# Full-width PE shapes, other FFN step budgets and a rotated PSUM set for the last FFN pair, in a fused attention and SwiGLU kernel

## The chip, the cores and the metric

One Trainium2 chip; the program runs on one of its cores. A time is device microseconds of one launch, the median of several executions. The engines are named as the profile names them: PE (TensorE's matmuls; PEld is its weight loads), ACT (ScalarE), DVE (VectorE), POOL (GpSimd, which here also issues the loads of q, k and v) and SP (which issues the loads of the weights and the stores of the result).

## The reference, cut to what matters

Causal attention with a decay from a running sum, on 8 batches with 8 heads of 576 rows and 64 columns, and then a normalised SwiGLU feed-forward layer (FFN) on the 4608 rows of 512 columns that the heads give together.

```python
scores = (1 / np.sqrt(64)) * q @ k.transpose(0, 1, 3, 2)
cum = np.cumsum(np.maximum(s, 0.0), axis=-1)
scores = np.where(causal, -1e9, scores + np.minimum(-(cum[..., :, None] - cum[..., None, :]), 0.0))
x = (softmax(scores) @ v).transpose(0, 2, 1, 3).reshape(4608, 512)
xn = x / np.sqrt(np.mean(x * x, axis=-1, keepdims=True) + 1e-06) * rms_g
g, val = xn @ w_gate, xn @ w_val            # 512 x 1536 each
out = (g / (1 + np.exp(-g)) * val) @ w_out  # 1536 x 512
```

## The kernel before, in words

The 64 heads n (8 of each batch) are written in a loop (lines 298 to 316). A row of 576 is cut in five chunks, four of 128 and one of 64 (`CS`, line 19). For each head:

- `emit_load` (157): POOL issues three loads (q, k, v) into one of three fixed staging tiles, two heads ahead. A load reads 640 rows, so it takes 64 rows of the next head too (not so for the last head).
- `emit_te` (178), one head ahead: ten transposes on PE (185, 187) put q and k into PSUM with 65 rows; the row more carries the running sum. DVE copies qt (190), ACT copies kt (191), 576 columns each.
- `emit_spv` (194): for each chunk jb of keys, the scores (209; their columns are the queries from 128·jb on: 512 and 64, 448, 320, 192, 64), exp on ACT into `pt` (211), and a select on POOL that zeroes the upper triangle of the diagonal block (214). Scores have two PSUM buffers ("s"). Then for each of five chunks i of queries the value matmuls (222), 15 in all, with `pt` as the loaded operand and v as the 65 moving columns; the last column gives the denominators. DVE inverts these (228) and scales into the x tile of the batch (229). For the last chunk jb = 4 only 64 rows are used, and for i = 4 only 64 columns are loaded.

After the eighth head of a batch, `emit_batch_tail` (233) normalises its five x tiles on DVE, with a logarithm and an exp on ACT. After every second batch a generator `ffn_pair_steps` (248) is queued, which writes the FFN of two batches (T = 1152 rows) in 55 steps: 10 transposes of x (257, 260); 36 gate steps, which for each of 12 blocks fb of 128 hidden columns take the rows in groups of 512, 512 and 128 (four matmuls for the gate into pg, 267; tanh on ACT, 270; four for the value into pvl, 273; on DVE uscr = (tanh + 1)·pg, 276, and h = uscr·pvl, 279); and 9 output blocks of 12 matmuls into py (286), a copy on ACT (289) and a store (290). pg, pvl and py share two PSUM buffers ("f"). The loop writes four steps after each head while a generator is queued; what is left is written after the last head.

What is written is not the order on the chip: a planner in the framework orders each engine's instructions when the kernel is compiled, by its own costs and by what is ready, and it takes what is written earlier first. Each engine then runs its instructions in that fixed order, and waits by semaphores. Buffers of a pool tile are handed on when all who use them are done.

## Time and profile before

| | before |
|---|---|
| median of 4 runs | 622.77 us (622.17 to 622.98) |
| profiled execution, and its span | 622.17 us; 620.4 us |
| PE busy, share of the span | 520.1 us, 84% |
| DVE | 350.9 us, 57% |
| ACT | 325.4 us, 52% |
| POOL | 257.6 us, 42% |
| chain that ended last | PE 47%, issue 15%, POOL 13%, ACT 11%, DVE 9% |
| granted TensorE clock, mean | 0.952 of 2.4 GHz |

The span counts from the first instruction to the last; the profiled execution took 1.8 us more than it. Busy time of PE is modelled at its end (matmuls overlap), so single matmuls look longer (379 ns on average for an output matmul) than the distance between two of them. The chain of waits goes back from the last instruction, at each step to what released it; "issue" is time in which an engine waited for nothing that the profile shows. No engine's share tells what bounds the kernel, since the stages differ: heads alone, gate steps beside heads, output blocks, and a last FFN pair alone.

### The profile page before, as it was taken

How to read it: one execution, taken by the hardware profiler on the slowest of the kernel's cores; microseconds unless marked ns; L12 is line 12 of the kernel's file. 1: busy time of each engine (PE TensorE's matmuls, PEld its weight loads, DVE VectorE, ACT ScalarE, POOL GpSimd, SP SyncE). 2: the span in 40 equal slices, each digit the busy share in tenths (PEclk: the TensorE clock that was granted, in tenths of full speed). 3: DMA queues.
4: the chain of work that ended last, by engine and by line, in shares of the span. 5: the costliest groups of instructions: out<-in, count | busy, mean ns of one | idle time of the engine just before them, and what ended most of it. 6: DMA issues, size and time to landing. Idle time of an engine off the chain costs nothing.

```text
span 620.4 us, 10789 instructions
## 1 busy us (share of the span) xinstructions
PE 520.1 (84%) x3733; PEld 290.8 (47%) x3733; DVE 350.9 (57%) x1261; ACT 325.4 (52%) x671; POOL 257.6 (42%) x523
## 2 busy tenths in 40 slices
PE   0078878979999999799989998799989995777797
PEld 0045555545555545455545545455545452333343
DVE  5345565667787703767877407667877126555510
ACT  2475676656676624656676426467766342222221
POOL 4167768665565503475565306465563010000000
PEclk9999999989998998789989997699989996999999
DMA  9997759556555535285556425465552220000012
GB/s 244 295 173 50 49 36 61 33 38 40 38 36 36 39 90 90 17 54 33 39 33 40 60 102 50 27 44 34 38 36 14 71 86 0 2 0 2 0 57 97
DMA packets 134534, 35.42 MB, mean 57 GB/s; under 512 B 127248, under 2 KB 127248, under 8 KB 134480
## 3 DMA queue, kind: packets, MB, share of 16 engines
q0 software_dynamic: 125808, 15.72, 40.3%
q1 hardware_dynamic: 8672, 19.03, 8.7%
q8 instruction: 29, 0.48, 0.3%
q14 instruction: 25, 0.20, 0.1%
HBM read 40.99 MB, written 9.44 MB: 81 GB/s over the span
## 4 chain that ended last, share of the span: by engine, by line
PE 47%; issue 15%; POOL 13%; ACT 11%; DVE 9%; DMA 4%; POOLq 0%; SPq 0%; DVEq 0%; ACTq 0%
PE pg L267 14%; PE pvl L273 8%; PE py L286 8%; PE ps L209 6%; PE pv L222 5%; POOL stk L176 4%; DVE uscr L276 4%; ACT tscr L270 4%; POOL pt L214 4%; ACT pt L211 3%; POOL stq L176 3%; DMA wgs<-in_moe_w_gate_dram 3%; POOL stv L176 2%; PE pq L185 2%; PE pk L187 2%
## 5 line engine op out<-in xcount | busy, mean ns | idle before, releaser
L211 ACT ACTIVATE pt<-ps,cum_T 128x512 bf16<-128x512 f32 (+5 forms) x384 | 170.9, 479 | 92.2 <-PE ps L209 86.1
L267 PE MATMUL pg<-xT,wg_sb 128*128 128x512 bf16 (+1 forms) x576 | 126.6, 339 | 12.8 <-DVE uscr L276 12.0
L214 POOL TENSOR_SCALAR_AFFINE_SELECT pt<-pt 128x128 bf16<-128x128 bf16 (+1 forms) x320 | 91.0, 304 | 93.8 <-ACT pt L211 90.9
L273 PE MATMUL pvl<-xT,wv_sb 128*128 128x512 bf16 (+1 forms) x576 | 120.6, 332 | 5.1 <-DVE h L279 4.9
L209 PE MATMUL ps<-qt,kt 65*128 65x512 bf16 (+5 forms) x384 | 107.4, 323 | 17.7 <-ACT pt L211 16.0
L276 DVE SCALAR_TENSOR_TENSOR uscr<-tscr,pg 128x512 bf16<-128x512 bf16 x144 | 79.5, 552 | 71.5 <-ACT tscr L270 70.4
L228 DVE RECIPROCAL invden<-pv 128x1 f32<-128x1 f32 (+1 forms) x320 | 47.8, 161 | 124.6 <-PE pv L222 116.7
L270 ACT ACTIVATE tscr<-pg 128x512 bf16<-128x512 f32 x144 | 70.4, 489 | 89.6 <-PE pg L267 81.2
L222 PE MATMUL pv<-stv,pt 128*128 128x65 bf16 (+2 forms) x960 | 100.4, 215 | 18.7 <-POOL pt L214 12.7
L222 PEld LDWEIGHTS <-pt 128*128 128x128 bf16 (+2 forms) x960 | 67.8, 112 | 80.5 <-POOL pt L214 26.3
L286 PE MATMUL py<-wo_sb,h 128*128 128x512 bf16 x432 | 93.9, 379 | 0.0
L176 POOL DMA_DIRECT2D stq<-in_q_dram x63 | 54.6, 867 | 88.2 <-DVE stq L167 75.7
L229 DVE TENSOR_SCALAR x<-pv,invden 128x64 bf16<-128x64 f32 (+1 forms) x320 | 82.1, 275 | 1.8
L279 DVE TENSOR_TENSOR h<-uscr,pvl 128x512 bf16<-128x512 bf16 x144 | 78.5, 545 | 6.3 <-PE pvl L273 3.7
L273 PEld LDWEIGHTS <-wv_sb 128*128 128x128 bf16 x576 | 52.1, 100 | 58.1 <-issue 15.0
L267 PEld LDWEIGHTS <-wg_sb 128*128 128x128 bf16 x576 | 50.8, 100 | 56.5 <-issue 28.8
L176 POOL DMA_DIRECT2D stv<-in_v_dram x63 | 54.7, 867 | 42.3 <-PE ps L209 23.5
L176 POOL DMA_DIRECT2D stk<-in_k_dram x63 | 54.8, 869 | 26.5 <-PE pk L187 14.2
L286 PEld LDWEIGHTS <-h 128*128 128x128 bf16 x432 | 42.2, 98 | 50.1
L289 ACT ACTIVATE ysb<-py 128x512 f32<-128x512 f32 x36 | 21.5, 597 | 72.6 <-PE py L286 72.6
L185 PE MATMUL pq<-ident_bf,stq 128*65 128x128 bf16 x320 | 40.3, 251 | 12.4 <-DMA stq<-in_q_dram 10.5
L191 ACT ACTIVATE kt<-pk 65x576 bf16<-65x576 bf16 x64 | 40.9, 639 | 15.6 <-PE pk L187 12.1
(51 smaller groups left out, 333.8 us busy)
## 6 DMA issues: line engine op xcount, KB each, us to landing
out_dram<-ysb SPq DMA_DIRECT2D x36, 256.0 KB, 2.0
stk<-in_k_dram POOLq DMA_DIRECT2D x63, 80.0 KB, 2.9
stv<-in_v_dram POOLq DMA_DIRECT2D x63, 80.0 KB, 2.9
stq<-in_q_dram POOLq DMA_DIRECT2D x63, 80.0 KB, 2.9
wgs<-in_moe_w_gate_dram SPq DMA_DIRECT2D x4, 768.0 KB, 5.4
wvs<-in_moe_w_val_dram SPq DMA_DIRECT2D x4, 768.0 KB, 6.5
wos<-in_moe_w_out_dram SPq DMA_DIRECT2D x12, 256.0 KB, 6.4
cumB<-in_s_dram SPq DMA_DIRECT2D x1, 144.0 KB, 7.9
```

Source lines behind the costliest of these rows:

```text
L176: nc.gpsimd.dma_start(out=st[:, :, 0:D], in_=_head_src_ap(src, n, True))
L209: nc.tensor.matmul(ps[0:cs, 0 : a1 - a0], lhsT=kt[:, i0 : i0 + cs], rhs=qt[:, a0:a1], start=True, stop=True)
L211: nc.scalar.activation(out=pt[0:cs, OFF[jb] + a0 - i0 : OFF[jb] + a1 - i0], in_=ps[0:cs, 0 : a1 - a0], func=AF.Exp, bias=cum_T[0:cs, jb, n ...
L214: nc.gpsimd.affine_select(out=pt[0:cs, OFF[jb] : OFF[jb] + cs], in_=pt[0:cs, OFF[jb] : OFF[jb] + cs], pattern=[[1, cs]], compare_op=ALU.is ...
L222: nc.tensor.matmul(pv[0:ti, :], lhsT=pt[0 : CS[jb], OFF[jb] + 128 * (i - jb) : OFF[jb] + 128 * (i - jb) + ti], rhs=stv[0 : CS[jb], jb, :], ...
L229: nc.vector.tensor_scalar(out=x_tiles[b][i][0:ti, h * D : (h + 1) * D], in0=pv[0:ti, 0:D], scalar1=invden[0:ti, :], scalar2=None, op0=ALU. ...
L267: nc.tensor.matmul(pg[:, 0:gw], lhsT=wg_sb[:, cc, fb * 128 : (fb + 1) * 128], rhs=xT[:, cc, g0:g1], start=(cc == 0), stop=(cc == N_CC - 1))
L270: nc.scalar.activation(out=tscr[:, 0:gw], in_=pg[:, 0:gw], func=AF.Tanh, scale=0.5)
L273: nc.tensor.matmul(pvl[:, 0:gw], lhsT=wv_sb[:, cc, fb * 128 : (fb + 1) * 128], rhs=xT[:, cc, g0:g1], start=(cc == 0), stop=(cc == N_CC - 1))
L276: nc.vector.scalar_tensor_tensor(out=uscr[:, 0:gw], in0=tscr[:, 0:gw], scalar=1.0, in1=pg[:, 0:gw], op0=ALU.add, op1=ALU.mult)
L279: nc.vector.tensor_tensor(out=h_tiles[fb][:, g0:g1], in0=uscr[:, 0:gw], in1=pvl[:, 0:gw], op=ALU.mult)
L286: nc.tensor.matmul(py, lhsT=h_tiles[fc][:, t0 : t0 + 128], rhs=wo_sb[:, fc, :], start=(fc == 0), stop=(fc == N_FC - 1))
```

## The change

Four things are changed. First, PE's shapes: `pt` becomes two fixed tiles with 64 zeroed columns at the end, kt gets all 640 columns, the scores, exp and the value matmuls of the last chunk use 128 rows and columns, with the select still zeroing the rows that don't belong, and x is transposed in full 128 x 128 blocks (its last 64 rows are set to zero once for each batch). Second, in `ffn_steps` the narrow group of 128 rows keeps pg and pvl in one PSUM buffer, and its tanh comes after both. Third, with `deep`, which holds for the last pair alone, pg, pvl and py take their buffers in turn from "f", "s" and "pv". Fourth, the steps are written in two places, two units ahead of `emit_spv` and two after the head (two more if a second generator is queued, and two more from head 48 on); an output block counts as two units. Lines that stay are left out:

```diff
--- before.py
+++ after.py
@@ -148,6 +148,10 @@
                 for i in range(NCH)] for b in range(B)]
...
     h_tiles = [hpool.tile([128, SP], BF16, name=f"h_{fc}", tag=f"h_{fc}") for fc in range(N_FC)]
+
+    pt_slots = [const.tile([128, PT_W + 64], BF16, name=f"pt{s}") for s in range(2)]
+    for s in range(2):
+        nc.vector.memset(pt_slots[s][:, PT_W : PT_W + 64], 0.0)
...
     teed = {}
@@ -186,18 +190,18 @@
         for c in range(NCH):
...
         qt = work.tile([65, S], BF16, name="qt", tag="qt", bufs=2)
-        kt = work.tile([65, S], BF16, name="kt", tag="kt", bufs=2)
+        kt = work.tile([65, NCH * 128], BF16, name="kt", tag="kt", bufs=2)
         nc.vector.tensor_copy(out=qt, in_=pq[:, 0:S])
-        nc.scalar.activation(out=kt, in_=pk[:, 0:S], func=AF.Copy)
+        nc.scalar.activation(out=kt, in_=pk, func=AF.Copy)
         teed[n] = (qt, kt)
...
         stq, stk, stv = staged.pop(n)
-        pt = work.tile([128, PT_W], BF16, name="pt", tag="pt", bufs=2)
+        pt = pt_slots[n % 2]
         for jb in range(NCH):
-            cs = CS[jb]
+            cs = 128
             w = WID[jb]
...
             if jb == 0:
@@ -212,17 +216,17 @@
                                      in_=ps[0:cs, 0 : a1 - a0],
...
             nc.gpsimd.affine_select(
-                out=pt[0:cs, OFF[jb] : OFF[jb] + cs], in_=pt[0:cs, OFF[jb] : OFF[jb] + cs],
-                pattern=[[1, cs]], compare_op=ALU.is_ge, fill=0.0,
+                out=pt[0:cs, OFF[jb] : OFF[jb] + CS[jb]], in_=pt[0:cs, OFF[jb] : OFF[jb] + CS[jb]],
+                pattern=[[1, CS[jb]]], compare_op=ALU.is_ge, fill=0.0,
                 base=0, channel_multiplier=-1)
...
                 nc.tensor.matmul(
-                    pv[0:ti, :],
-                    lhsT=pt[0 : CS[jb], OFF[jb] + 128 * (i - jb) : OFF[jb] + 128 * (i - jb) + ti],
-                    rhs=stv[0 : CS[jb], jb, :],
+                    pv,
+                    lhsT=pt[:, OFF[jb] + 128 * (i - jb) : OFF[jb] + 128 * (i - jb) + 128],
+                    rhs=stv[:, jb, :],
                     start=(jb == 0), stop=(jb == i))
...
             nc.vector.reciprocal(out=invden[0:ti, :], in_=pv[0:ti, 64:65])
@@ -245,80 +249,105 @@
                 out=x_tiles[b][i][0:ti, :], in0=x_tiles[b][i][0:ti, :],
...
-    def ffn_pair_steps(bp):
-        b0 = 2 * bp
-        xT = work.tile([128, N_CC, SP], BF16, name="xT", tag="xT", bufs=2)
-        for half in range(2):
+    def ffn_steps(batches, deep=False):
+        b0 = batches[0]
+        T = len(batches) * S
+        cg_list = [(0, 512), (512, 1024), (1024, T)] if T > 1024 else [(0, 512), (512, T)]
+        rot = [0]
+
+        def fpsum(nm):
+            if deep:
+                tg = ("f", "s", "pv")[rot[0] % 3]
+                rot[0] += 1
+            else:
+                tg = "f"
+            return psum.tile([128, 512], FP32, name=nm, tag=tg, bufs=2)
+
+        xT = work.tile([128, N_CC, T], BF16, name="xT", tag="xT", bufs=2)
+        for bi, bb in enumerate(batches):
             for i in range(NCH):
                 ti = CS[i]
-                off = half * S + C0[i]
+                off = bi * S + C0[i]
                 ptr = psum.tile([128, N_CC, 128], BF16, name="ptr", tag="ptrans", bufs=2)
                 for cc in range(N_CC):
-                    nc.tensor.transpose(ptr[:, cc, 0:ti],
-                                        x_tiles[b0 + half][i][0:ti, cc * 128 : (cc + 1) * 128],
-                                        ident_bf[0:ti, 0:ti])
+                    nc.tensor.transpose(ptr[:, cc, :],
+                                        x_tiles[bb][i][:, cc * 128 : (cc + 1) * 128],
+                                        ident_bf)
                 nc.vector.tensor_copy(out=xT[:, :, off : off + ti], in_=ptr[:, :, 0:ti])
-                yield
+                yield 1
         for fb in range(N_FC):
-            for (g0, g1) in CG:
+            for (g0, g1) in cg_list:
                 gw = g1 - g0
-                pg = psum.tile([128, 512], FP32, name="pg", tag="f", bufs=2)
+                one = gw <= 256
+                pg = fpsum("pg")
                 for cc in range(N_CC):
...
                 tscr = work.tile([128, 512], BF16, name="tscr", tag="tscr", bufs=2)
-                nc.scalar.activation(out=tscr[:, 0:gw], in_=pg[:, 0:gw], func=AF.Tanh, scale=0.5)
-                pvl = psum.tile([128, 512], FP32, name="pvl", tag="f", bufs=2)
+                if one:
+                    pvl = pg[:, 256 : 256 + gw]
+                else:
+                    nc.scalar.activation(out=tscr[:, 0:gw], in_=pg[:, 0:gw], func=AF.Tanh, scale=0.5)
+                    pvl = fpsum("pvl")
                 for cc in range(N_CC):
...
                                      rhs=xT[:, cc, g0:g1], start=(cc == 0), stop=(cc == N_CC - 1))
+                if one:
+                    nc.scalar.activation(out=tscr[:, 0:gw], in_=pg[:, 0:gw], func=AF.Tanh, scale=0.5)
                 uscr = work.tile([128, 512], BF16, name="uscr", tag="uscr", bufs=2)
...
                                         in1=pvl[:, 0:gw], op=ALU.mult)
-                yield
-        for tb in range(N_TB):
-            t0 = tb * 128
-            py = psum.tile([128, D_MODEL], FP32, name="py", tag="f", bufs=2)
+                yield 1
+        for t0 in range(0, T, 128):
+            tw = min(128, T - t0)
+            py = fpsum("py")
             for fc in range(N_FC):
-                nc.tensor.matmul(py, lhsT=h_tiles[fc][:, t0 : t0 + 128],
+                nc.tensor.matmul(py[0:tw, :], lhsT=h_tiles[fc][:, t0 : t0 + tw],
                                  rhs=wo_sb[:, fc, :], start=(fc == 0), stop=(fc == N_FC - 1))
             ysb = work.tile([128, D_MODEL], FP32, name="ysb", tag="ysb", bufs=2)
-            nc.scalar.activation(out=ysb, in_=py, func=AF.Copy)
-            nc.sync.dma_start(out=out[b0 * S + t0 : b0 * S + t0 + 128, :], in_=ysb)
-            yield
+            nc.scalar.activation(out=ysb[0:tw, :], in_=py[0:tw, :], func=AF.Copy)
+            nc.sync.dma_start(out=out[b0 * S + t0 : b0 * S + t0 + tw, :], in_=ysb[0:tw, :])
+            yield 2
+
+    ffn_gens = []
+
+    def run_ffn_steps(budget):
+        while budget > 0 and ffn_gens:
+            try:
+                budget -= next(ffn_gens[0])
+            except StopIteration:
+                ffn_gens.pop(0)
...
     emit_te(0)
-    ffn_gens = []
-    FFN_STEPS_PER_HEAD = 4
     for n in range(B * H):
...
         emit_te(n + 1)
+        if n < B:
+            nc.vector.memset(x_tiles[n][NCH - 1][64:128, :], 0.0)
+        run_ffn_steps(2)
         emit_spv(n)
...
         if n % H == H - 1:
-            emit_batch_tail(n // H)
-            if (n // H) % 2 == 1:
-                ffn_gens.append(ffn_pair_steps((n // H) // 2))
-        steps = FFN_STEPS_PER_HEAD
-        while steps > 0 and ffn_gens:
-            try:
-                next(ffn_gens[0])
-                steps -= 1
-            except StopIteration:
-                ffn_gens.pop(0)
-    while ffn_gens:
-        try:
-            next(ffn_gens[0])
-        except StopIteration:
-            ffn_gens.pop(0)
+            b = n // H
+            emit_batch_tail(b)
+            grp = {1: [0, 1], 3: [2, 3], 5: [4, 5], 7: [6, 7]}.get(b)
+            if grp is not None:
+                ffn_gens.append(ffn_steps(grp, deep=(b == B - 1)))
+        end_budget = 2
+        if len(ffn_gens) > 1:
+            end_budget += 2
+        if n >= 6 * H:
+            end_budget += 2
+        run_ffn_steps(end_budget)
+    run_ffn_steps(1 << 30)
```

## Rows read from the trace of the kernel before

**Rows 1.** Windows by stage: us, busy of each engine, PEclk, DMA share, GB/s.

```profile
31.00:115.00 84.00, 70.38 (x499) 44.65 (x498) 45.98 (x207) 54.56 (x116) 62.23 (x125) 1.00 0.82 71
115.00:135.00 20.00, 16.91 (x140) 10.77 (x138) 14.34 (x60) 12.80 (x25) 9.92 (x22) 0.91 0.33 22
135.00:214.00 79.00, 73.60 (x611) 41.86 (x609) 59.72 (x216) 53.19 (x117) 47.85 (x94) 0.98 0.63 41
214.00:241.00 27.00, 26.94 (x155) 13.24 (x153) 3.71 (x15) 8.76 (x18) 2.08 (x7) 1.00 0.32 85
241.00:269.00 28.00, 22.84 (x182) 14.74 (x179) 18.23 (x77) 16.19 (x34) 15.77 (x32) 0.70 0.49 39
523.00:592.70 69.70, 52.87 (x281) 24.69 (x280) 38.17 (x69) 17.06 (x35) 0.00 (x0) 0.97 0.00 1
```

**Rows 2.** Chain of waits, tail, one triple: start us, us, what.

```profile
533.37 0.93 PE pg L267 x4
...
534.33 0.61 ACT tscr L270
...
534.96 0.70 DVE uscr L276
...
535.70 1.04 PE pg L267 x4
...
538.18 0.70 DVE h L279
...
539.31 0.93 PE pg L267 x4
```

**Rows 3.** Chain of waits, whole span, its longest pieces.

```profile
217.52 23.34 issue
...
522.67 1.86 PE pg L267 x4
...
592.70 23.38 PE py L286 x108
```

**Rows 4.** Groups: xcount | busy us, mean ns | idle before; loads by shape.

```profile
L276 DVE SCALAR_TENSOR_TENSOR uscr<-tscr,pg 128x512 bf16<-128x512 bf16 x144 | 79.5, 552 | 71.5 <-ACT tscr L270 70.4
L279 DVE TENSOR_TENSOR h<-uscr,pvl 128x512 bf16<-128x512 bf16 x144 | 78.5, 545 | 6.3 <-PE pvl L273 3.7
...
L222 PEld LDWEIGHTS <-pt 128*128 128x128 bf16 x640 | 46.0, 109 | 55.1 <-POOL pt L214 26.3 <-DVE x L229 8.8 <-issue 6.9
...
L191 ACT ACTIVATE kt<-pk 65x576 bf16<-65x576 bf16 x64 | 40.9, 639 | 15.6 <-PE pk L187 12.1 <-PE ps L209 3.0
...
L222 PEld LDWEIGHTS <-pt 128*64 128x64 bf16 x256 | 14.7, 122 | 21.0 <-issue 7.8 <-DVE x L229 4.8 <-DVE stq L167 3.1
```

**Rows 5.** Groups by line and shape, PE's loads, 135 to 214 us.

```profile
L273 PEld LDWEIGHTS <-wv_sb 128*128 128x128 bf16 x132 | 11.9, 100 | 12.4 <-issue 1.8
...
L209 PEld LDWEIGHTS <-kt 65*64 65x64 bf16 x11 | 1.2, 106 | 2.3 <-issue 1.9
```

**Rows 6.** Chain of waits, gate stage: start us, us, what.

```profile
155.54 0.39 PE pv L222 x5
...
158.80 0.22 PE pg L267 x4
...
174.60 0.22 PE pv L222 x7
```

**Rows 7.** Timeline, gate stage: start us, us, engine, line, operation, count.

```profile
151.97 0.11 PEld L209 LDWEIGHTS <-kt 65*64 65x64 bf16 x1 [0.42 <-issue]
151.97 0.22 PE L209 MATMUL ps<-qt,kt 65*64 65x64 bf16 x1
...
152.12 0.40 PE L222 MATMUL pv<-stv,pt 128*128 128x65 bf16 x7
...
154.51 1.03 PE L273 MATMUL pvl<-xT,wv_sb 128*128 128x512 bf16 x4
...
155.47 0.46 PE L222 MATMUL pv<-stv,pt 128*64 128x65 bf16 x5
```


## The prediction

> **What bounds the kernel now.** I read the stage table first [rows 1]: it cuts the span where the work changes, and the reader is to see that no one engine bounds all of it. Then the chain of waits in the last stage [rows 2], then the three long pieces of the whole chain [rows 3], then groups by line for durations and counts [rows 4, 5], and last the chain and the timeline inside one FFN stage for what narrow matmuls cost [rows 6, 7].
>
> - Heads without FFN work (31 to 115 us). POOL works 62 of 84 us, PE's matmuls leave gaps, the chain goes through POOL's loads and selects. POOL has 8 instructions a head (5 selects, 3 loads): 125 / 8 = 15.6 heads, 5.4 us each.
> - Gate stage (135 to 214): gate/value steps run beside heads; PE busy 73.6 of 79, DVE 59.7. It occurs three times. It holds 132 matmuls of the value projection, 12 for three steps (one fb, which I call a triple), and 11 narrow scores, one a head [rows 5]: 11 triples and 11 heads, 79 / 11 = 7.2 us for one of each.
> - Output stage (214 to 241), also three times: PE is busy 26.9 of 27 us, DVE 3.7, POOL 2.1. The chain has one piece of 23.34 us here [rows 3]: all nine output blocks, 108 matmuls, in a row, while the attention stands still. Heads without FFN work follow (241 to 269: 28 us, 32 POOL instructions, four heads, clock 0.70).
> - Tail. The fourth pair of batches runs alone: gate steps from 523 to 592.7, PE busy 52.9 of 69.7, then 108 output matmuls in 23.38 us [rows 3], 216 ns each and dense. In the gate part the chain [rows 2] goes pg, tanh on ACT, uscr on DVE, next pg: with two "f" buffers, a step's gate matmuls wait until the step before has left its buffer. One triple takes 539.31 - 533.37 = 5.94 us.
>
> **The change, part by part.** All sums are made against the profiled execution, 622.17 us (span 620.4 and 1.8 outside it), 0.1% below the median of 622.77.
>
> *Tail buffers.* The last pair takes PSUM in turn from "f", "s" and "pv": six buffers where there were two. A triple holds five accumulation buffers with the shared narrow one, so a buffer comes back more than one triple later, and the wait for uscr goes. What is late next is PE itself. Its work for a triple: 16 matmuls of 512 columns at 216 ns and 8 of 128 columns at 55 ns (four in 0.22 us [rows 6]), 3.46 + 0.44 = 3.90 us. DVE's: 3 x (0.552 + 0.545) = 3.29 us [rows 4], 84% of that, and it is the next limit. Twelve triples: 46.8 us. The first eight matmuls ran at the lower clock level, 1.2 GHz, after PE had been idle (1.86 us for four [rows 3], where four at 216 ns take 0.86); I keep that, +2.0. So 48.8 us against 592.70 - 522.67 = 70.0: **-21.2**. Bounds: nothing gained, if the planner keeps the old order; 2.04 x 12 + 2 = 26.5 if the slow start goes too.
>
> In the Trainium skill, "TensorE: Matmul & The Clock Gate", section Back-to-back issue gap, gives a sustained spacing of about 131 ns at 512 columns and 81 ns at 128 for load-and-matmul pairs. By that page a triple's matmuls would take 2.74 us, DVE's 3.29 would bind, and the tail would lose 7 us more. The trace has 216 ns over 108 dense pairs, so I don't use it.
>
> *Narrow matmuls made full.* Per head five of 15 value matmuls load 64 columns (one of them 64 rows), and one score matmul loads 64. In the chain, five of the narrow kind take 0.39 us where seven full ones take 0.22 [rows 6]: 78 against 31 ns, so five full ones are 0.16 and 0.23 is saved. The narrow score waits: its load stands idle 0.42 us on nothing but issue, and the next matmul starts 0.15 us after it [rows 7], where 0.03 would do by the 31 ns above. Entering costs too: the narrow values start 0.96 us after a pvl group of four that fills 0.86 [rows 7]; 0.1 for each of the two narrow groups. Sum: 0.23 + 0.12 + 0.2 = 0.55 us a head, 35 us over 64 heads if PE were the bound everywhere; zero is the other end.
>
> A rule of the Trainium skill speaks against this edit: "TensorE: Matmul & The Clock Gate", LDWEIGHTS, has the load's time go with its columns (P / 1.2 ns), so six loads a head that grow from 64 to 128 columns would add 6 x 53 ns, 20 us in all if loads were the bound. The trace's loads of 64 columns take 122 ns on average and those of 128 take 109 [rows 4]: nothing to lose.
>
> Where it counts: in the gate stage PE needs 3.90 for the triple and for the head ten transposes (0.56, as the 128-column matmuls), 1600 score columns (0.68), 15 value matmuls (0.47) and the 0.55: 6.2 of the 7.2 us. After: 5.6, about as long as the triple's own chain of 5.94, which the narrow step shortens: its value matmuls no longer wait for h in another buffer (up to 0.3). I let 0.5 a pair through: 11 x 0.5 = 5.5 for each of two gate stages, and half in the third, where what is not done beside it is done later: **-14**. Elsewhere the chain is POOL's: 0.15 for 16 first heads and for 8 later ones: **-3.6**. Bounds of this part: 0 and -35.
>
> *FFN steps before and after the head, output blocks counted double.* In the first three pairs the rate of gate steps is the same as before (four a head; six from head 48), but output blocks are written two a head instead of four. Why do nine run in one block now? POOL's counts (125 + 22 + 94 = 241 by 214 us, less six loads that run two heads ahead, over 8) put PE at head 29 when the gate steps end, while they are written by head 26: FFN work lags by nearly three heads, and PE takes what is written earlier first. After the change the blocks are written from 27 to 31, so of nine about five are due when the gate steps end and still run in a row; the other four fall beside heads 29 to 31. A head alone has 5.4 - 2 = 3.4 us of free PE, and a block takes 2.6: 3 to 4 blocks hide, 9 us at most, I take 7 for the first two pairs: **-14**. Bounds: 0 (all nine due at once) and 15 a pair (no lag: 4.5 heads x 3.4). In the third pair six units a head write the blocks by head 58, so all nine are due at once as now: 0.
>
> *Added work.* kt is copied with 640 columns for 576 (639 ns now [rows 4]): 64/576 of it at most, 0.07 us a head, on an ACT that is busy 53 of 79 us in the gate stage and 55 of 84 before [rows 1]; it feeds the next head, so that head hides it; without cover 4.5 us. Exp and select of the last chunk get more partitions, not more columns: 0. Eight memsets of x and two of the pad on DVE, which waits for PE in the first heads: 0; at most 10 x 0.55, the price of a whole uscr step [rows 4]. pt as two fixed tiles: still two, released by the same last matmul: 0. The pv that reads 64 columns of the next chunk waits for a select that the next matmul needs anyway, and what is queued behind it on PE waits no longer than now: 0. A moved output block takes its copy on ACT and its store on SP with it; SP issues nothing else by then, and POOL's queue has none of these: 0. Narrow steps with tanh after both matmuls: 0.22 us later for ACT, hidden by five other buffers in the tail, and by heads elsewhere.
>
> Sum: -21.2 - 14 - 3.6 - 14 = -52.8, 622.2 - 52.8 = **569.4 us**.
>
> **Rivals.**
> 1. *Output blocks stay in one block.* For it: PE takes earlier-written work first, and the 23.34 us show it. Against: two blocks a head are written much later than now. 569.4 + 14 = 583.
> 2. *Shape changes bought nothing in the gate stage*, since the chain of tanh and uscr (5.94) binds there and not PE. 569.4 + 14 = 583; with rival 1, only the tail and little else: 600.
> 3. *More goes:* no lag, a tail that also starts at full clock, the narrow cost returned wherever a head runs: 569.4 - 16 - 5 - 5 = 543.
> 4. *Slower:* FFN steps written ahead of spv go ahead of its scores on PE's in-order queue. For it: the output stage, where heads stand still for 23 us. Place: the 33 heads of three gate stages; price: a wide step's eight matmuls, 1.73 us a head, uncovered: 33 x 1.73 = 57; the blocks stay together and the other gains remain (-21 - 18): 622 + 18 = 640. It decides from 39 / 33 = 1.2 us a head. Against: in the gate stage the seven values, then a head's other work, stand between one group of pvl and the next pg [rows 6, 7].
> 5. *The tail doesn't do what it says* (buffers are still taken two at a time): 569.4 + 21 = 590.
>
> **How the numbers follow.** Forecast 0.54; rival 1 or 2 alone 0.22 (583); both, 0.06 (600); rival 3 0.09; rival 5 0.04; rival 4 0.05. The forecast's own spread is 555 to 582. The range 544 to 602 holds it, rivals 1, 2 (alone and together) and 5, and reaches the edge of 3. This kernel's measurement tells 0.2% (1.2 us) from no change. Only rival 4 has times above 622: slower 0.04, same 0.02, faster 0.94.
>
> **What would show it.** Tail: the gate part near 49 us, PE waiting nowhere for uscr, DVE over 80% busy in it; wrong, if a triple stays above 5 us. Shapes: no issue idle before value loads, full forms alone in the value groups, gate stages of 73 us or less; wrong, if they keep 79. Output: the long chain piece breaks into one of some 13 us and shorter ones with selects between, in two stages, and stays 23 in the third; wrong, if it is whole. The forecast as a whole is wrong if heads in the gate stage take longer than 7.2 us.

## The result, and the profile after

The changed kernel takes 576.17 us (median of 11 runs, 573.13 to 577.72) where the kernel before takes 622.64 (16 runs): a ratio of 0.9246, with an interval of 0.9227 to 0.9265. That is 46.5 us less; the forecast was 52.8 less, 569.4 us. The profiled execution took 577.67 us with a span of 575.6, so it is among the longer runs; against the profiled execution of before (622.17) it is 44.5 us less. The mean granted clock is the same, 0.953 against 0.952.

The windows by stage, of the changed kernel, cut at the same events as [rows 1] (us; busy time of PE, PEld, DVE, ACT, POOL with counts; PEclk; DMA share; GB/s):

```profile
31.00:115.00 84.00, 62.03 (x504) 42.12 (x503) 45.59 (x210) 57.09 (x119) 63.05 (x128) 1.00 0.82 70
115.00:134.60 19.60, 14.28 (x128) 9.31 (x127) 13.33 (x56) 13.16 (x27) 10.15 (x22) 0.74 0.38 25
134.60:205.80 71.20, 67.31 (x595) 39.43 (x592) 59.22 (x205) 49.08 (x107) 42.31 (x82) 1.00 0.61 39
205.80:235.00 29.20, 28.95 (x196) 14.14 (x195) 8.14 (x39) 12.74 (x28) 11.56 (x23) 1.00 0.58 97
235.00:258.50 23.50, 18.28 (x179) 12.44 (x176) 17.16 (x69) 16.54 (x34) 14.53 (x28) 0.85 0.61 49
501.50:548.30 46.80, 46.80 (x281) 23.84 (x280) 36.34 (x68) 16.79 (x34) 0.00 (x0) 0.96 0.00 1
```

Read the third to the fifth row against those of [rows 1] by POOL's counts, eight of which are a head. Before, 94, 7 and 32 POOL instructions ran in 79, 27 and 28 us: 133 in 134.0 us. After, 82, 23 and 28 run in 71.2, 29.2 and 23.5 us: again 133, in 123.9 us. So the same 16.6 heads with the same FFN work take 10.1 us less, but the gate stage, 7.8 us shorter, takes 12 POOL instructions fewer along, a head and a half; the output stage takes 16 more, two heads.

The tail, in the chain of waits of the changed kernel (start us, us, what), answers to [rows 2]:

```profile
513.21 0.86 PE pg L284 x4
514.07 0.86 PE pvl L293 x4
514.93 0.86 PE pg L284 x4
515.80 0.86 PE pvl L293 x4
516.66 0.22 PE pg L284 x4
516.88 0.22 PE pg L293 x4
517.11 0.86 PE pg L284 x4
```

Nothing but PE is in it: a triple takes 517.11 - 513.21 = 3.90 us for 5.94, and ACT and DVE have left the chain. In the row of the tail above, PE is busy for all of its 46.80 us.

The output blocks, in the whole chain of the changed kernel, answer to [rows 3]; the pieces of the first and the third pair, the tail's first matmuls and the last pair's blocks are shown:

```profile
205.84 7.84 PE py L308 x36
...
217.12 2.59 PE py L308 x12
...
224.65 2.59 PE py L308 x12
...
232.17 2.59 PE py L308 x12
...
451.44 23.33 PE py L308 x108
...
501.48 1.71 PE pg L284 x4
...
548.31 23.32 PE py L308 x108
```

In [rows 3] the piece of 23.34 us of pair 1 is named issue: the chain runs there through POOL, which waits for nothing that the profile shows. That the nine blocks fill this time is seen on PE, in the timeline of the kernel before:

```profile
216.17 23.47 PE L286 MATMUL py<-wo_sb,h 128*128 128x512 bf16 x108
```

This row is now one of 7.84 us (three blocks), a fourth in pieces and a fifth that ends at 217.12 + 2.59 = 219.71; then come whole blocks 7.5 us apart, each with the next one in pieces between a head's matmuls behind it. In the third pair all nine still run in a row.

Narrow forms are gone. In the chain of the gate stage, seven and five value matmuls (of [rows 6] the last and the first):

```profile
172.04 0.23 PE pv L226 x7
...
174.58 0.16 PE pv L226 x5
```

And PE's loads in the gate stage, by line and shape (busy us, mean ns | idle before, and its cause), which answer to [rows 4, 5]:

```profile
L293 PEld LDWEIGHTS <-wv_sb 128*128 128x128 bf16 x140 | 11.8, 97 | 10.3 <-issue 1.3
L226 PEld LDWEIGHTS <-pt 128*128 128x128 bf16 x150 | 8.5, 98 | 6.8 <-POOL pt L218 1.1 <-DVE x L233 0.7 <-issue 0.3
L213 PEld LDWEIGHTS <-kt 65*128 65x128 bf16 x59 | 5.2, 98 | 2.7 <-issue 0.3
```

The idle time on issue before the narrow score's load, 1.9 us over 11 heads in [rows 5], is 0.3 over all 59 score loads. The counts say the same as POOL's: 140 loads for the value projection are 11.7 triples, 150 of `pt` are 10 heads, in 71.2 us. Before it was 11 triples and 11 heads in 79. So the stage takes 6.1 us for each triple that it holds, where it took 7.2; for each head it takes 7.1, where it took 7.2.

### The profile page after: what moved, and what is told of

Read it like the earlier page. It is cut to its first block, busy times and chain, and to the rows that moved or that the text cites. A ratio compares the mean times of both kernels' runs of the same rounds, so it can differ in the third digit from the quotient of the medians.

```text
span 575.6 us, 10935 instructions
## 1 busy us (share of the span) xinstructions
PE 483.1 (84%) x3733; PEld 276.6 (48%) x3733; DVE 354.6 (62%) x1271; ACT 327.0 (57%) x671; POOL 260.6 (45%) x523
## 4 chain that ended last, share of the span: by engine, by line
PE 54%; ACT 12%; POOL 11%; issue 9%; DVE 8%; DMA 5%; ACTq 0%; SPq 0%; POOLq 0%; DVEq 0%
PE py L308 16%; PE pg L284 13%; PE pvl L293 9%; ACT pt L215 5%; PE ps L213 5%; PE pv L226 4%; POOL pt L218 4%; POOL stk L180 3%; DMA wgs<-in_moe_w_gate_dram 3%; DVE uscr L298 3%; PE pq L189 2%; POOL stv L180 2%; POOL stq L180 2%; DMA stq<-in_q_dram 2%; PE pk L191 2%
## 5 line engine op out<-in xcount | busy, mean ns | idle before, releaser
L215 ACT ACTIVATE pt<-ps,cum_T 128x64 bf16<-128x64 f32 (+4 forms) x384 | 170.6, 480 | 60.5 <-PE ps L213 44.0
L284 PE MATMUL pg<-xT,wg_sb 128*128 128x512 bf16 (+1 forms) x576 | 123.6, 334 | 2.4 <-DVE uscr L298 0.8
L213 PE MATMUL ps<-qt,kt 65*128 65x64 bf16 (+4 forms) x384 | 105.4, 321 | 17.7 <-ACT pt L215 15.7
L226 PE MATMUL pv<-stv,pt 128*128 128x65 bf16 x960 | 89.9, 212 | 23.4 <-POOL pt L218 18.8
L226 PEld LDWEIGHTS <-pt 128*128 128x128 bf16 x960 | 65.5, 109 | 87.6 <-POOL pt L218 43.2
L293 PE MATMUL pvl<-xT,wv_sb 128*128 128x512 bf16 x384 | 103.1, 389 | 0.4 <-DVE h L301 0.4
L308 PE MATMUL py<-wo_sb,h 128*128 128x512 bf16 x432 | 99.2, 379 | 0.0
L290 ACT ACTIVATE tscr<-pg 128x512 bf16<-128x512 f32 x96 | 57.2, 596 | 59.7 <-PE pg L284 52.1
L180 POOL DMA_DIRECT2D stv<-in_v_dram x63 | 55.8, 885 | 39.7 <-PE pv L226 17.5
L301 DVE TENSOR_TENSOR h<-uscr,pvl 128x512 bf16<-128x512 bf16 x96 | 64.9, 676 | 2.4
L195 ACT ACTIVATE kt<-pk 65x640 bf16<-65x640 bf16 x64 | 44.5, 695 | 23.6 <-PE pk L191 23.2
```

What stands on the lines that cost most here:

```text
L180: nc.gpsimd.dma_start(out=st[:, :, 0:D], in_=_head_src_ap(src, n, True))
L213: nc.tensor.matmul(ps[0:cs, 0 : a1 - a0], lhsT=kt[:, i0 : i0 + cs], rhs=qt[:, a0:a1], start=True, stop=True)
L215: nc.scalar.activation(out=pt[0:cs, OFF[jb] + a0 - i0 : OFF[jb] + a1 - i0], in_=ps[0:cs, 0 : a1 - a0], func=AF.Exp, bias=cum_T[0:cs, jb, n ...
L226: nc.tensor.matmul(pv, lhsT=pt[:, OFF[jb] + 128 * (i - jb) : OFF[jb] + 128 * (i - jb) + 128], rhs=stv[:, jb, :], start=(jb == 0), stop=(jb ...
L284: nc.tensor.matmul(pg[:, 0:gw], lhsT=wg_sb[:, cc, fb * 128 : (fb + 1) * 128], rhs=xT[:, cc, g0:g1], start=(cc == 0), stop=(cc == N_CC - 1))
L290: nc.scalar.activation(out=tscr[:, 0:gw], in_=pg[:, 0:gw], func=AF.Tanh, scale=0.5)
```

## The experiments

Each ratio is against the kernel before on the same chip, with its 95% interval. First each part of the change was put into the kernel before by itself; then three of the parts were taken out of the changed kernel; then the shapes were split and the step budgets varied.

### The rotated buffers alone

Parts of its edit (pvl and py are changed as pg is):

```diff
+            if deep:
+                tg = ("f", "s", "pv")[rot[0] % 3]
...
-                pg = psum.tile([128, 512], FP32, name="pg", tag="f", bufs=2)
+                pg = fpsum("pg")
...
-                ffn_gens.append(ffn_pair_steps((n // H) // 2))
+                ffn_gens.append(ffn_pair_steps((n // H) // 2, deep=(n == B * H - 1)))
```

> The kernel before with one part of the change: the last pair takes pg, pvl and py in turn from the three PSUM tags (its narrow group keeps two buffers, so a triple takes six). Theory of the prediction, the tail waits for buffers and is then bound by PE: 12 triples of 3.90 us in place of 5.94, the gate part of the tail about 47 to 49 us for 70, the rest unchanged, 598 to 602 us. Rival, the wait for uscr has another cause than the buffers (tanh and DVE in order): within 5 us of 622. Rival, the lower clock takes part of it back: PEclk below 0.95 in the tail and 605 to 615.

Measured 599.98 us, 0.9616 [0.9572, 0.9659]: 22.7 us less. The chain of waits in its tail:

```profile
540.47 0.86 PE pg L277 x4
541.33 0.86 PE pvl L283 x4
542.20 0.86 PE pg L277 x4
543.06 0.86 PE pvl L283 x4
543.92 0.22 PE pg L277 x4
544.15 0.22 PE pvl L283 x4
544.37 0.86 PE pg L277 x4
```

A triple is 544.37 - 540.47 = 3.90 us, with six buffers a triple and nothing shared. So the rotation alone gives the tail its whole gain; the shared narrow buffer adds nothing there.

### The full shapes alone, and without them

Parts of its edit:

```diff
-        pt = work.tile([128, PT_W], BF16, name="pt", tag="pt", bufs=2)
+        pt = pt_slots[n % 2]
...
-            cs = CS[jb]
+            cs = 128
...
-                    pv[0:ti, :],
...
+                    pv,
```

> The kernel before with the full shapes alone (pt as two fixed tiles, kt of 640 columns, 128 rows and columns in the last chunk, full transposes of x with zeroed rows). Theory of the prediction, PE loses about 0.55 us a head at the changes between narrow and full shapes and half of it counts: 602 to 610 us, gate stages of 73 us for 79. Rival, the chain of tanh and uscr binds the gate stages and POOL the heads alone: 619 to 624. Rival by the load rule (time goes with the columns): six loads of 64 more columns a head, some us slower, 625 to 640.

Measured 605.23 us, 0.9705 [0.9671, 0.9739]: 17.5 less, where the prediction's two terms for the shapes make 17.6. All nine output blocks still run in a row here. The mean granted clock of its profiled execution is 0.971 for 0.952, so a part of the gain may be clock; no run separates the two.

> The changed kernel with the narrow shapes of before. Theory, the full shapes take 0.55 us of PE from each head and about half of it counts, as alone (17 us): 588 to 597 us, PE's issue pauses ahead of value loads are back. Rival, with the other parts PE has slack beside the heads: 576 to 583.

The changed kernel with the old shapes took 602.85 us, 0.9665 [0.9632, 0.9698]: 26.7 above the changed kernel, and more than I expected. The shapes are worth 9 us more beside the other parts than alone.

### The values alone, and the last score alone

Two kernels, each the kernel before with half of the shapes:

Parts of the edit for the values:

```diff
-        pt = work.tile([128, PT_W], BF16, name="pt", tag="pt", bufs=2)
+        pt = pt_slots[n % 2]
...
-                    pv[0:ti, :],
...
+                    pv,
```

And for the last score:

```diff
-        kt = work.tile([65, S], BF16, name="kt", tag="kt", bufs=2)
+        kt = work.tile([65, NCH * 128], BF16, name="kt", tag="kt", bufs=2)
...
-                nc.tensor.matmul(ps[0:cs, 0 : a1 - a0], lhsT=kt[:, i0 : i0 + cs],
+                nc.tensor.matmul(ps[:, 0 : a1 - a0], lhsT=kt[:, i0 : i0 + 128],
```

> The kernel before with full shapes for the value matmuls alone (pt as two fixed tiles, rows and columns of the last chunk that no exp writes zeroed once); the last score stays 64 wide. Theory, PE pays at each change between a narrow and a full shape: of 0.55 us a head 0.33 belong to the values, so 60% of the 17 us of the full shapes: 610 to 614 us, no issue pause ahead of value loads, one still ahead of the narrow score. Rival, it is the single load or the fixed tiles and not the change of shape: all 17 us, 603 to 608, or nothing, 619 to 624.

> The kernel before with a full last score alone (kt copied with 640 columns, the score written to 128 rows of which exp still reads 64); the value matmuls stay narrow. Theory, 0.22 of 0.55 us a head: 614 to 619 us. Rival, the score's pause is covered by exp and tanh, and the longer copy of kt costs: 621 to 626.

Values: 612.93 us, 0.9846 [0.983, 0.9862]. Score: 612.92 us, 0.9838 [0.9814, 0.9862]. Each gives nearly 10 us, and together they gave 17.5; for the score I had expected less (614 to 619). The fixed tiles of `pt` come with the full values and were not tried by themselves. The loads of `kt` in the gate stage of the kernel with full values alone show its price again:

```profile
L213 PEld LDWEIGHTS <-kt 65*128 65x128 bf16 x50 | 4.0, 101 | 0.8
L213 PEld LDWEIGHTS <-kt 65*64 65x64 bf16 x10 | 1.1, 106 | 2.2 <-issue 1.9
```

The ten narrow ones stand idle 1.9 us on issue; of the 0.8 us before the fifty full ones the row puts nothing down to it.

The gain of the full score is not spread over the heads, though. Its profiled execution gains 0.4 us up to the first value matmul of head 18, 0.2 from there to that of head 34, 6.1 from there to that of head 50, and 1.6 from there to the tail. The windows of the third of these stretches, of the kernel before and of this one:

```profile
268.40:401.40 133.00, 123.28 (x935) 69.32 (x932) 81.38 (x305) 77.59 (x165) 64.19 (x128) 0.92 0.52 49
```

```profile
267.80:394.70 126.90, 117.47 (x933) 66.86 (x932) 80.59 (x303) 77.13 (x165) 62.82 (x127) 0.96 0.52 49
```

The granted clock is 0.96 here for 0.92. In the stretch before it, with 16 heads too, it is 0.91 for 0.92, and next to nothing is gained. So these 10 us are not a price that was paid once a head, and how much of them is the clock stays open.

### The shared narrow buffer alone, and without it

```diff
-                nc.scalar.activation(out=tscr[:, 0:gw], in_=pg[:, 0:gw], func=AF.Tanh, scale=0.5)
-                pvl = psum.tile([128, 512], FP32, name="pvl", tag="f", bufs=2)
+                one = gw <= 256
+                if one:
+                    pvl = pg[:, 256 : 256 + gw]
+                else:
+                    nc.scalar.activation(out=tscr[:, 0:gw], in_=pg[:, 0:gw], func=AF.Tanh, scale=0.5)
+                    pvl = psum.tile([128, 512], FP32, name="pvl", tag="f", bufs=2)
...
+                if one:
+                    nc.scalar.activation(out=tscr[:, 0:gw], in_=pg[:, 0:gw], func=AF.Tanh, scale=0.5)
```

> The kernel before with the narrow group of 128 rows in one PSUM buffer and its tanh after both products, nothing else. Theory, the narrow step's value matmuls no longer wait for h (0.4 us in a triple of the tail) and the next gate matmuls wait a bit instead: 0.2 to 0.3 us of 48 triples, 608 to 619 us. Rival, the later tanh costs what the wait gave: 621 to 624. The planner may also end the gate steps earlier, so that fewer heads lie beside them.

Measured 634.16 us, 1.0171 [1.0133, 1.0208]: 11.5 us more. I had forecast it to cost nothing and to save up to 0.3 us a triple. In the tail it does save; its chain of waits there, one triple:

```profile
547.73 1.04 PE pg L267 x4
...
549.41 0.70 DVE uscr L282
...
550.15 1.04 PE pg L267 x4
...
552.64 0.70 DVE h L285
...
553.38 1.04 PE pg L267 x4
```

553.38 - 547.73 = 5.65 us for 5.94. The loss lies beside the heads. From the first value matmul of head 18 to that of 34 takes 140.2 us (133.4 before), from there to 50 136.4 (133.0), and from there to the tail's first step 126.8 (121.2): 15.8 us more, less 3.8 in the tail, 12.0. The windows up to the first output block of pair 1, of the kernel before and of this one:

```profile
31.00:216.10 185.10, 162.93 (x1265) 98.66 (x1264) 121.72 (x488) 122.24 (x262) 120.61 (x241) 0.98 0.68 53
```

```profile
31.00:212.60 181.60, 161.25 (x1222) 96.80 (x1221) 120.68 (x473) 117.67 (x253) 115.71 (x231) 0.97 0.66 51
```

The gate steps end 3.5 us earlier, but with 231 POOL instructions done for 241: more than a head less. Its output blocks still run nearly in a row; the chain's piece there, six blocks:

```profile
212.73 15.54 PE py L292 x72
```

The heads that are left over run after them, and cost more there than the 5.4 us of the first stage: the stretch behind the output blocks takes 7.0 us a head in the kernel before (28.0 us, 32 POOL instructions, granted clock 0.70 [rows 1]) and 7.4 in this one (34.0 us, 37, clock 0.60, from 240.80 on). One and a quarter heads at 7.0, less the 3.5 us, make 5.3 of the 6.8 us that the first stretch lost. So faster gate steps are no gain if they leave heads behind that run with nothing beside them.

> The changed kernel with pg and pvl of the narrow group in two buffers again and its tanh between them; the rest of the change stays. Theory from the single parts (the narrow sharing alone cost 11 us: 15 lost beside the heads, 4 won in a tail that waits for buffers): with six buffers the tail has nothing to win from it, so without it the kernel is faster, 560 to 568 us, gate stages with one head more beside them. Rival, the loss came from that one schedule and not from the sharing: 574 to 579. Rival, the tail of six accumulations a triple waits for buffers again: gate part above 50 us in the tail.

Without the sharing the changed kernel took 577.69 us, 0.926 [0.9236, 0.9284]: the same as with it. My theory that the sharing cost the changed kernel 8 us or more, so that 560 to 568 would come out, fell.

What the sharing does to the order is the same wherever it is put in. When the first output block of pair 1 begins, 421 to 423 value matmuls are done (15 a head, so 28.1 to 28.2 heads) in each of the six kernels here that have the sharing, and 438 or 450 (29.2 or 30.0 heads) in each of the eight that don't. The windows up to that block for the tile `pv` alone (busy time of PE and DVE with counts), of the changed kernel and of the one without the sharing:

```profile
0.00:205.70 205.70, 42.77 (x421) 55.10 (x280) 0.98 0.75 86
```

```profile
0.00:211.30 211.30, 45.07 (x450) 58.65 (x298) 0.97 0.77 86
```

So the sharing takes one to two heads out of the gate stage. In return fewer blocks run in a row at its end: 36 matmuls in the changed kernel, over 80 without the sharing.

### The step budgets alone, and without them

```diff
+        run_ffn_steps(2)
         emit_spv(n)
-        steps = FFN_STEPS_PER_HEAD
+        end_budget = 2            # +2 with two generators, +2 from head 48
+        run_ffn_steps(end_budget)
-            yield                 # an output block
+            yield 2
```

> The kernel before with the FFN steps in two places of a head, an output block counted as two units and two units more from head 48, nothing else. Theory of the prediction, nine output blocks no longer stand in one row in the first two pairs: about 7 us each, 605 to 612 us, the long chain piece of 23 us broken into one of 11 to 16 us and single blocks. Rival 1, heads that ran beside the gate steps now run alone and take it back: 619 to 624. Rival 4, FFN steps go ahead of a head's scores: above 630.

Measured 614.82 us, 0.9863 [0.9826, 0.9899]: 7.9 us less, and less than I expected of it. The chain's longest pieces of output blocks:

```profile
219.35 12.98 PE py L286 x60
...
233.58 4.64 PE py L286 x21
...
344.53 15.54 PE py L286 x72
```

Five and six blocks run in an unbroken row, where the changed kernel has three in pair 1 and two in pair 2 (5.24 us, 24 matmuls).

> The changed kernel with four FFN steps after each head, none ahead of spv, and an output block counted as one. Theory, as alone (8 us): 582 to 588 us, output blocks in rows of six and three. Rival, the blocks' place is worth nothing once the heads are cheaper: 574 to 579.

The changed kernel with four steps after the head took 594.65 us, 0.9514 [0.9476, 0.9553]: the budgets are worth 18.5 us there, more than the 6 to 12 that I expected.

### Without the two extra steps from head 48 on

```diff
-        if n >= 6 * H:
-            end_budget += 2
```

> The changed kernel without the two units more from head 48 on. Theory, nine output blocks of the third pair stand in one row because they are written by head 58; written from 59 to 63 they break up as in the first two pairs: 568 to 573 us, the 23 us piece of the chain gone. Rival, the heads at the end have then fewer bare stretches but the last batch's values come later, and the tail starts as late as now: 575 to 578.

Measured 571.1 us, 0.9148 [0.9115, 0.9181]: 5 us less than the changed kernel. From the first value matmul of head 48 on, where the edit begins to act, the profiled execution takes 203.0 us for 208.5. The third pair's blocks break up as those of the others do; the chain's first pieces there:

```profile
452.88 4.61 PE py L308 x21
...
457.54 3.19 PE py L308 x14
...
461.89 1.94 PE py L308 x9
...
471.63 2.54 PE py L308 x11
```

> The changed kernel without the two units more from head 48 and without the shared narrow buffer. By the single differences (5 us less and 1.5 more): 570 to 575 us. Rival, the sharing is what lets the gate steps end early enough for the blocks to break up, so that seven of them stay in one row in the third pair: 574 to 579.

Without the sharing as well it took 575.48 us, 0.9239 [0.922, 0.9258], 4.4 more, and 84 matmuls (seven blocks, 18.13 us) run in a row in the first and in the third pair. Here the sharing, which cost 11.5 us alone, is a gain: the gate steps end so early that fewer blocks are due (421 value matmuls are done when the first one begins in pair 1, for 450).

### Fewer steps at the end

```diff
-        if n >= 6 * H:
-            end_budget += 2
+        if 6 * H <= n < 6 * H + 6:
+            end_budget -= 1
```

> The changed kernel without the two units more from head 48, and with one unit less after heads 48 to 53, so that two output blocks of the third pair are left for the time after the last head. Theory, PE stands idle some 5 us there while the last batch is normalised, and its clock falls; two blocks of 2.6 us fill that: 564 to 568 us, against 571. Rival, the blocks then go ahead of the last batch's transposes and push the tail back: 570 to 574.

Measured 566.51 us (566.03 to 567.94), 0.9105 [0.9088, 0.9123]: the fastest version, 9.7 us below the changed kernel; that it beats the one without the extra steps is not settled, since their intervals touch. The traces do not bear it out: from the first value matmul of head 48 on, this kernel's profiled execution takes 202.5 us, the other's 203.0. Its lead was there earlier. PE's matmuls stand in the same order in the changed kernel and in this one up to that point, yet the two reach it at 367.1 and 361.8 us, with a mean granted clock of 0.953 and 0.976 over their whole spans. So, by these executions, some 6 us of the gain over the changed kernel come from this edit, and next to nothing beyond what leaving out the extra steps gave.

Two of the third pair's blocks are now left for the time after the last head's values, where PE waited for the last batch's normalisation. PE in the changed kernel (timeline; idle time before it in brackets), and in this one:

```profile
498.42 1.04 PE L273 MATMUL ptr<-ident_bf,x 128*128 128x128 bf16 x8 [5.45 <-DVE x L248]
```

```profile
479.65 3.83 PE L308 MATMUL py<-wo_sb,h 128*128 128x512 bf16 x17
...
486.52 2.11 PE L273 MATMUL ptr<-ident_bf,x 128*128 128x128 bf16 x16 [2.59 <-DVE xT L276]
```

The gap is 2.59 us for 5.45. But from the last value matmul to the last batch's transposes PE now takes 8.2 us (478.30 to 486.52) for 5.45; in the chain a block's copy on ACT (0.60 us at 480.98) stands ahead of the normalisation. Of the two blocks (24 matmuls, 5.2 us, from 478.3 on) about half ran in time that was idle before.

## Why the prediction was right, and where it was off

**Tail: right.** Forecast -21.2 with a gate part of 48.8 us; it is 46.8, and the rotation alone gave -22.7. The 3.90 us a triple came out to the digit. I counted twelve triples after a slow start; one wide step was already done before the last batch's normalisation, in both kernels. The slow start remains, as I kept it: 1.71 us for the first four matmuls. DVE is busy 36.3 of 46.8 us, 78%, a little under the 80% I named. With 0.86 us for four matmuls of 512 columns over the whole tail, the spacing is 216 ns. The 131 ns that the Trainium skill gives ("TensorE: Matmul & The Clock Gate", Back-to-back issue gap) would have put DVE in the chain; no DVE step is in it.

**Shapes: right in size alone, but not in all of the working.** Forecast -17.6, alone -17.5, with a higher granted clock. The values' five matmuls take 0.16 us as worked out, and the loads lost nothing by growing (98 ns in the gate stage). The 78 ns that I gave each narrow value matmul is a mean that hides where the time goes. In the gate stage of the kernel before, two narrow ones of one shape start 36 ns apart and two full ones 30 (medians of 32 pairs each with no wait between); it is the matmul after the one of 64 rows, or after the narrow score, that starts 119 to 147 ns later (three pairs). For the score I had 0.22 us a head beside 0.33 for the values. Alone both gave the same, but the score's gain came nearly whole in one stretch with a higher clock, so its price a head stays open. That the size came out alone is thus in part luck. The Trainium skill's rule that a load's time goes with its columns ("TensorE: Matmul & The Clock Gate", LDWEIGHTS) would have made the shapes cost; two kernels and their rows speak against it here.

**Output blocks: right in kind.** I read the 23.34 us of [rows 3] as the nine blocks, where the row says issue; PE's timeline bears the reading out. The blocks spread in pairs 1 and 2 and not in the third, as I argued from the lag of PE behind the written order; in pair 1 three run in an unbroken row and five are done 13.9 us after the first began, where I had five in a row of 13 us, and four fall beside heads, as I had them. That the third pair stays whole because of its six units a head was shown by taking two of them away: the blocks broke up, and 5 us came with it.

**Added work: right where it was on its own, wrong for the shared buffer.** The copy of kt went from 639 to 695 ns and the eight memsets of x cost 2.2 us of DVE in all, before 12 us of the span; none is in the chain. The sharing I put at nothing or a little gain. Alone it costs 11.5 us, in the whole nothing, and without the extra steps it gains 4.4. What I left out is that it ends the gate steps with one to two heads fewer beside them.

**The mis-sized term: what a faster gate stage is worth in the first two pairs.** For the period from head 18 to 34, and 34 to 50, I had 13.1 us each: 5.5 for the gate stage, 7 for the blocks, 0.6 for four later heads. The periods went from 133.4 and 133.0 to 123.9 and 123.5: 9.5 each, and twice 3.6 is 7.2 of the 8.3 us that the profiled runs fall short (44.5 of 52.8). The first heads (-0.4 where I had 16 x 0.15 = 2.4) and the third period (-1.9 for 2.8) lack 2.9 more, and the tail gave 1.9 back. These smaller differences are no larger than those between executions: the changed kernel and the two that are written alike up to head 48 reach head 18 at 134.6, 133.1 and 130.6 us. The period from head 18 to 34 is 123.6 to 123.9 us in all three. The step that failed is the one that held eleven heads in the gate stage and took 0.5 us from each pair of triple and head. In fact the stage fell by 1.1 us for each of its triples and hardly at all for each of its heads: by the windows above it came out 7.8 us shorter where I let 5.5 through, and ran 10 heads for 11. The shared buffer takes them out, as the counts of value matmuls in six kernels with it and eight without show. The head and a half left over come after the stage, at more than the 5.4 us that I took for a head alone (7.0 a head behind the output blocks before, 6.7 after: 23.5 us, 28 POOL instructions), and so the stretch from the end of the gate steps to the next gate stage got 2.3 us shorter (52.7 for 55.0) where I had 7.6. A head in the gate stage takes 7.1 us, just under the 7.2 beyond which I would have called the whole forecast wrong.

**The parts don't add up.** Alone they give -22.7, -17.5, +11.5 and -7.9, in sum 586 us; measured 576. Take one part out, and the three others nearly add up: without shapes 603.6 by sums and 602.85 measured, without the budgets 594.0 and 594.65, without sharing 574.6 and 577.7. A kernel without the rotation alone was not run. The four together depart by 10 us. By these sums the sharing's loss is gone once both full shapes and spread blocks are there; the two pairs of kernels that differ in the sharing alone beside both (577.69 and 576.17, 575.48 and 571.1) agree with it. That the heads which its shorter gate stage leaves over then have blocks beside them fits with the windows and the counts, but why spread blocks with narrow shapes don't do the same stays open.

Of the rivals none came true. Nine blocks in one row, as rival 1 has them, are left in the third pair alone, where I had them; rival 4 fell: the matmuls of wide steps are not queued in front of the scores at 1.7 us a head, as the same 133 POOL instructions in 10 us less show.

## What to carry to other kernels

When one queue of work runs beside another, ask of each saving which of the two it speeds up: if only the one that ends first, what is left of the other runs bare, and the saving can come back as a cost unless something else is written there. Work that can be put anywhere (here the output blocks) belongs beside what would run bare; whether filling a gap such as the last normalisation with it pays, the runs here don't settle. Writing such work faster only made it due all at once here. And test a part both alone and taken out of the whole: here one part was +11.5, 0 and -4.4 us. Before a gain is put down to an edit, see where in the span it falls: here 5.3 us of the fastest version's lead stood ahead of its edit.

## What the runs showed of the hardware

- A load of 64 columns is no shorter than one of 128: 122 ns and 109 before [rows 4], 98 for the full ones in the gate stage after. The price of a narrow matmul is in the change of shape: two narrow value matmuls in a row start 36 ns apart, the matmul after a change 119 to 147 (three pairs), and there is an idle 1.9 us on issue over ten or eleven loads, in both kernels with the narrow score whose rows are shown, and 0.3 over all 59 score loads of the changed kernel.
- A gain divided by its heads is not yet a price a head. With one full score a head in place of a narrow one the kernel took nearly 10 us less (ratio 0.9838), but 6.1 of them fell in one stretch of 16 heads with a granted clock of 0.96 for 0.92, and 0.2 in another of 16 heads with 0.91 for 0.92.
- Executions differ where nothing was changed. The kernel before and the one with the rotation alone have the same order of PE's matmuls, and reach head 18 at 135.0 and 137.3 us; the changed kernel and the fastest have the same order up to head 48, and reach it at 367.1 and 361.8. A stretch of a single profiled execution is known to a few us.
- PE's granted clock is not full after the idle time here, and is higher where other matmuls fill it. Windows of 10 us over the last normalisation, of the changed kernel and of the fastest:

```profile
490.00:500.00 10.00, 3.87 (x33) 2.31 (x31) 7.93 (x29) 4.41 (x7) 0.82 (x2) 0.67 0.00 0
```

```profile
480.00:490.00 10.00, 7.32 (x51) 4.61 (x49) 5.04 (x16) 4.15 (x6) 0.00 (x0) 0.83 0.16 60
```

With PE busy 7.32 us for 3.87 the granted clock is 0.83 for 0.67. What ran ahead of the two windows differs too (nine blocks in a row up to 474.77 us in the one, blocks between heads up to 478 us in the other), so the two blocks are not all that differs. Of the matmuls of 512 columns after it only the first two take 0.43 us in the fastest kernel's chain, where eight do in the changed kernel's (1.71 us for four, twice).
